# Gated linear attention and a gated SSM block: empty TensorE instructions behind 14 matmuls instead of 24, alpha's transpose ahead of the masks, v loaded ahead of q

## The chip, the cores and the metric

The kernel runs on one core of a Trainium2 chip. The metric is the device time of one execution in microseconds. A core has five engines with an instruction stream each, which meet only at semaphores: PE (TensorE, matmuls; its loads of the stationary operand are shown as PEld), DVE (VectorE), ACT (ScalarE), POOL (GpSimd) and SP (SyncE, which issues DMAs here). PE writes its results to PSUM, eight banks; DVE and ACT read them there.

## The reference, cut to what matters

Four batches, 8 heads, 768 steps, 48 channels a head. An attention with a state that decays by alpha, then a projection to two halves, a scan over one, a gate by the other, and an output projection.

```python
for t in range(S):
    state = alpha[:, :, t, :, None] * state + np.einsum('bhd,bhe->bhde', k[:, :, t], v[:, :, t])
    y[:, :, t] = np.einsum('bhd,bhde->bhe', q[:, :, t], state)
# x = y as (B, S, H * D)
proj = x @ w_in
val, gate = (proj[..., :D_inner], proj[..., D_inner:])
for t in range(S):
    h = a[0, 0] * h + val[:, t, :]
    ys[:, t, :] = h
silu = gate * (1.0 / (1.0 + np.exp(-gate)))
return (silu * ys @ w_out)
```

## The kernel before

The steps are cut into 12 groups of 256 (three for each batch), and a group is the unit of the outer loop in `fast`, `for n in range(N)`. The order on every engine is written out by hand: each engine runs its instructions in the order in which the Python code makes them, and there is no scheduler. A second function, `general`, is a way out for inputs that `fast` does not cover; it does not run here.

Three groups are in work in a turn n of the loop (for n from 2 on): the projection, gate and output of group n, the attention of group m = n + 1, and the preparation and the scores of group m + 1.

- **Preparation (DVE), `products`, lines 674 to 691.** A generator whose steps are taken one by one by `go(1)`: transpose alpha (`turn("a")`, tile al), transpose k, scan P of running products, scan V of the inverse ones (with `junk` on ACT), Zk = k x V, transpose q, Zq = q x P. `turn` is line 613.
- **Scores (PE), `scores`, line 816,** 64 matmuls of 64 x 112 from Zk and Zq into two pairs of PSUM banks, and **`masks`, lines 820 to 835:** DVE masks the first of each pair (A), ACT copies the second (AK) and the rest of the first (K), and POOL masks AK. ACT's copy K of a bank waits until DVE's mask of the same bank is done, and the second AK stands behind the first K on ACT.
- **Attention (PE), `third` and what surrounds it:** `carried` (L862), `values` (L849) and, for the next group, `states` (L881), which reads AK and K. `join` copies the result (ACT, L977, L978) and moves it between partitions by eight DMAs, four on SP's and four on POOL's queue, into xT.
- **Projection (PE), `project`, lines 997 to 1033:** four column blocks cc, six fp32 matmuls each (three for the value half, three for the gate half), all L1010; the scan hh on DVE (L1019) needs the first three of its block. The fourth scan is kept back (`late=True`) until Zq has been made, and behind it, with `f3`, stand the scores and masks of the group after.
- **Output (PE), `output_parts`,** 14 matmuls (L1095), whose sums are on DVE, POOL and ACT.

**Empty instructions.** Behind each projection matmul `project` puts `fill(n, cc, i)` instructions `nop` on PE (L1013). They compute nothing. `FILL` says how many there are for each group, and `fill` spreads them over the 24 matmuls:

```python
FILL = {1: 78, 2: 79, 3: 128, 4: 128, 5: 96, 6: 128, 7: 128, 8: 96, 9: 128}
count = FILL.get(n, 0)
at = 2 * NK * cc + i
return count * (at + 1) // 24 - count * at // 24
```

**Loads.** `load_raw` brings q, k or alpha of a group by four DMAs on SP's queue into one buffer for each of the three, so a load waits for the transpose that reads the buffer last. `load_v` brings v by two DMAs into one of two buffers in turn. SP issues in order: in a turn first the moves of `join`, then q, alpha, then in the next turn k, the output rows of the turn before and v.

Of the kernel before, what the change touches and what calls it, by code (L numbers as in the profile page):

```python
# [342 lines left out]
FIRST_PRODUCT = 1e18  # L343
FLOOR = 1e-31
FILL = {1: 78, 2: 79, 3: 128, 4: 128, 5: 96, 6: 128, 7: 128, 8: 96, 9: 128}


@with_exitstack
def fast(
# [25 lines left out]
    nc = tc.nc  # L375
# [7 lines left out]
    N = B * NG  # L383
# [50 lines left out]
    def load_v(m, engine):  # L434
        if m >= N:
            return
        b, g = divmod(m, NG)
        for c in range(G):
            if m:
                to = vs[m % NV][:, c, :, 0:D]  # L440
            else:
                to = wide[:, c].rearrange("p (h d) -> p h d", d=D)[:, ::2, :]
            engine.dma_start(out=to, in_=v[b, :, ds(g * GC + c * C, C), :].rearrange("h p d -> p h d"))
# [361 lines left out]
    def scores(m, cs=range(G)):  # L805
        Zk, Zq = Zks[m], Zqs[m % 2]
        for c in cs:
            scs.setdefault(m, []).append(bank_pair(None if c else "s"))
            if not c or not m:
                sts.setdefault(m, []).extend(scs[m][c])  # L810
            for p in range(4):
                for h in range(2):
                    u = 2 * c + h
                    for i in range(2):
                        rows = ds(64 * i, D)
                        nc.tensor.matmul(scs[m][c][i][ds(L * h, L), ds(p * (L + D), L + D)],  # L816
                                         Zk[rows, c, p, ds(h * L, L)], Zq[rows, u, p],
                                         start=True, stop=True, skip_group_check=True)

    def masks(m, cs=range(G)):  # L820
        sc = [[t[:, 0:4 * (L + D)].rearrange("p (h x) -> p h x", h=4) for t in pair] for pair in scs[m]]
        mb = mask[:, None, :]
        if m < NG:
            for c in cs:
                for i in range(2):
                    nc.vector.tensor_mul(As[i][:, c], sc[c][i][:, :, D:], mb.to_broadcast([C, 4, L]))
                for i in range(2):
                    nc.scalar.activation((K0, dS[m % 2][1])[i][:, c, :, 0:D], sc[c][i][:, :, 0:D], AF.Copy)
            return
        for c in range(G):  # L830
            nc.vector.tensor_mul(A0s[m % 2][:, c], sc[c][0][:, :, D:], mb.to_broadcast([C, 4, L]))
            nc.scalar.activation(AKs[m % 2][:, c], sc[c][1], AF.Copy)
            nc.scalar.activation(K0[:, c, :, 0:D], sc[c][0][:, :, 0:D], AF.Copy)
            t = AKs[m % 2][:, c, :, D:]
            nc.gpsimd.tensor_mul(t, t, mb.to_broadcast([C, 4, L]))
# [127 lines left out]
    for h in range(H):  # L963
        i, e, s = h // 4, h % 4 // 2, h % 2 ^ h // 4
        at = D * h
# [26 lines left out]
    def fill(n, cc, i):  # L992
        count = FILL.get(n, 0)
        at = 2 * NK * cc + i
        return count * (at + 1) // 24 - count * at // 24

    def project(n, cc, late=False, between=None):
        if cc == 0:
# [243 lines left out]
    for n in range(N):  # L1242
        m = n + 1
        if n == 0:
            V = scan_V(1, P)
            high(1)
            fs_late = [project(n, 0)]
            add_low(1)
            alphas(2)
            scaled_k(1, tk, V)  # L1250
            scaled_q(1, tq, P)
            low(2)
            fs_late.append(project(n, 1))
            convert(2)
            first(m)
            tk = straighten(2, "k")
            P = scan_P(2)
            tq = straighten(2, "q")
            V = scan_V(2, P)
            low(3)  # L1260
            convert(3)
            load_raw("k", 3, nc.sync)
            junk(1)
            def across_and_states():
                values(m, True)
                add_banks(m, states(m))

            f2 = project(n, 2, between=across_and_states)
            nc.scalar.activation(wobits[0][0:1, 0, 0, 0:1], minus[0:1], AF.Relu)
            load_w_out(0, nc.sync)  # L1270
            alphas(3)
            third(m)
            load_w_out(1, nc.sync)
            for name in "qa":
                load_raw(name, 3 + (name == "a"), nc.sync)
            load_v(3, nc.sync)
            for c in range(G):
                scaled_k(2, tk, V, c)
                scaled_q(2, tq, P, c)
        elif n == 1:  # L1280
            scores(m)
            masks(m)
            h3, f3 = project(0, 3, True)
            f2()
            P = scan_P(3)
            h3()
            values(m, True)
            st = states(m)
            add_banks(m, st)
            for f in fs_late:  # L1290
                f()
            f3()
            f0 = project(n, 0)
            convert(4)
            junk(2)
            low(5)
            convert(5)
            f1 = project(n, 1)
            f0()
            tk = plain("k")  # L1300
            turn("k", tk)
            third(m)
            load_raw("k", 4, nc.sync)
            load_v(4, nc.sync)
            f1()
            junk(3)
            V = scan_V(3, P)
            f2 = project(n, 2)
            scaled_k(3, tk, V)
            f2()  # L1310
            check_w(4)
            output(0)
            sum_weights()
            f3 = project(n, 3)
            tq = plain("q")
            turn("q", tq)
            load_raw("q", 4, nc.sync)
            scaled_q(3, tq, P)
            f3()
            go(2)  # L1320
        else:
            if n == 2:
                go(1)
            else:
                if m + 1 < N:
                    go(1)
                    load_raw("k", n + 3, nc.sync)
                go(1)
                next(outs, None)
                load_v(m + 1, nc.sync)  # L1330
            if n == N - 2:
                check_w(5)
            f0 = project(n, 0)
            f0()
            go(1)
            if n == 2:
                load_raw("a", n + 3, nc.sync)
                load_raw("k", n + 3, nc.sync)
            if n == N - 2:
                check_w(1)  # L1340
            f1 = project(n, 1)
            f1()
            sum_early()
            if n == 2:
                values(m, True)
                states(m)()
                add_up(m)
            if n == N - 2:
                check_w(2)
            go(1)  # L1350
            f2 = project(n, 2)
            f2()
            if n == N - 1:
                sum_last(0)
            if n == N - 2:
                check_end()
            go(1)
            if n == N - 1:
                tc.mark_branch_hint_location("last", hint=0, engines=[mybir.EngineType.PE, mybir.EngineType.Activation, mybir.EngineType.DVE, mybir.EngineType.SP, mybir.EngineType.Pool])
                value = nc.values_load(flag[0:1, 0:1], min_val=0, max_val=1)  # L1360
            h3, f3 = project(n, 3, True)
            if m + 1 < N:
                go(1)
            h3()
            f3()
            if m + 1 < N:
                scores(m + 1)
                masks(m + 1)
            if n == N - 3:
                check_w(3)  # L1370
            if n < N - 1:
                sum_late()
            else:
                sum_last(1)
            if m < N:
                rest = third(m)
                load_raw("q", n + 3, nc.sync)
                if m + 1 < N and m not in apart:
                    evict = states(m + 1)
                    values(m + 1, True)  # L1380
                go(1)
                if n + 3 < N:
                    load_raw("a", n + 4, nc.sync)
                rest()
                outs = output_parts(n)
                next(outs)
                if m + 1 < N and m not in apart:
                    evict()
                next(outs)
                if m in apart:  # L1390
                    values(m + 1, True)
                    states(m + 1)()
                if m + 1 < N:
                    add_up(m + 1)
            if n == N - 3:
                check_w(0)
        if n == N - 2:
            check_flag()
        if n == 1:
            output(n)  # L1400
            first(m + 1)
# [53 lines left out]
```

## Time and profile before

| | us |
|---|---|
| median of three runs | 284.66 |
| lowest and highest | 284.0, 284.67 |
| the profiled execution | 284.6 |
| its span, first to last instruction | 282.9 |
| busy: PE, PEld, DVE, POOL, ACT | 264.6, 232.7, 238.6, 158.9, 112.6 |
| the projections' matmuls L1010, into mm and into y | 103.6, 27.5 |

A busy PE is not a PE at its peak, since matmuls are pipelined and their ends are modelled. An fp32 matmul stands in the trace as two loads and two passes, so the 24 matmuls of one projection are x48. Instructions that only a sequencer handles, the empty ones among them, count as no engine's work: they are found by their line alone. "issue" is time in which an engine waited for nothing that the profile shows. One turn of the loop takes some 21 us; its scores start at 107.30, 128.86, 151.40, 172.23, 193.42, 215.70 and 236.52 us.

### The profile page before, as it was taken

To read this page: it belongs to the slowest core of one execution; us is meant where nothing else is said; L and a number is where in the kernel's file an instruction comes from. 1 tells how busy PE (TensorE), PEld (TensorE's weight loads), DVE (VectorE), ACT (ScalarE), POOL (GpSimd) and SP (SyncE) were. 2 spreads that over 40 slices of the span, in tenths; PEclk is the share of its full clock that TensorE was granted. 3 is DMA by queue.
4 is the path that set the end of the run, shared out by engine and by line. 5 is a ranking of instruction groups with operands and counts; after the bars stand their busy time and mean duration, and the time that the engine had idled before them with its cause. 6 is when DMAs were issued, how large, how long until landed. Compare 5 with 4: busy or idle time off the path is not lost.

```text
span 282.9 us, 11027 instructions
## 1 busy us (share of the span) xinstructions
PE 264.6 (94%) x4172; PEld 232.7 (82%) x4172; DVE 238.6 (84%) x326; ACT 112.6 (40%) x272; POOL 158.9 (56%) x195
## 2 busy tenths in 40 slices
PE   8999999999997997997997998997997997999995
PEld 6988888866786986986886987986886986988884
DVE  6979998998998898898698898898888988593452
ACT  3658665541524334334432533433423523414121
POOL 8122222445458884864695795775695795636110
PEclk9999999999999999999999999999999999999999
DMA  6937975989940693693594495594495460110201
GB/s 188 311 120 231 285 164 155 270 164 246 228 93 6 151 228 95 167 236 69 135 218 119 111 223 140 142 215 117 122 217 136 105 157 2 46 56 21 80 5 58
DMA packets 52308, 41.25 MB, mean 146 GB/s; under 512 B 27392, under 2 KB 50944, under 8 KB 52256
## 3 DMA queue, kind: packets, MB, share of 16 engines
q1 hardware_dynamic: 49472, 37.53, 54.9%
q0 software_dynamic: 1536, 2.20, 2.9%
q10 hardware_dynamic: 1248, 0.79, 1.0%
q8 instruction: 37, 0.61, 0.9%
q14 instruction: 15, 0.12, 0.1%
HBM read 32.54 MB, written 4.72 MB: 132 GB/s over the span
## 4 chain that ended last, share of the span: by engine, by line
PE 52%; DVE 30%; issue 6%; DMA 6%; ACT 2%; SPq 1%; POOL 1%; DVEq 0%; ACTq 0%; POOLq 0%
PE mm L1010 14%; PE mm L1095 14%; DVE q L613 6%; DVE V L667 6%; DMA raw_k<-in_k_dram 5%; DVE hh L1019 5%; DVE Zq L623 4%; PE s L816 3%; PE mm L816 3%; PE y L1095 3%; PE s L881 3%; PE y L862 2%; DVE P L648 2%; PE y L849 2%; DVE Zk L632 2%
## 5 line engine op out<-in xcount | busy, mean ns | idle before, releaser
L1010 PE MATMUL mm<-xT,w_in 128*128 128x256 f32 x456 | 103.6, 382 | 0.1
L1010 PEld LDWEIGHTS mm<-xT,w_in 128*128 128x128 f32 x456 | 85.5, 190 | 12.4 <-POOL w_in L569 0.4
L1032 POOL TENSOR_TENSOR f_last<-sg,hh 128x256 f32<-128x256 f32 x36 | 40.3, 1121 | 33.1 <-DVE hh L1019 21.9
L1030 ACT ACTIVATE sg<-mm 128x256 f32<-128x256 f32 x38 | 14.5, 382 | 84.3 <-PE mm L1010 84.3
L980 POOL DMA_DIRECT2D xT<-yst x44 | 22.5, 517 | 12.7 <-ACT yst L977 12.4
L667 DVE TENSOR_TENSOR_SCAN V<-al,ends 128x1028 f32<-128x1028 f32 x12 | 29.1, 2422 | 0.4
L648 DVE TENSOR_TENSOR_SCAN P<-al,lower 128x1028 f32<-128x1028 f32 x12 | 27.5, 2291 | 0.3
L1010 PE MATMUL y<-xT,w_in 128*128 128x256 f32 x120 | 27.5, 379 | 0.0
L1019 DVE TENSOR_TENSOR_SCAN hh<-a_dec,hh,mm 128x256 f32<-128x256 f32 x26 | 19.2, 738 | 8.1 <-PE mm L1010 8.1
L1010 PEld LDWEIGHTS y<-xT,w_in 128*128 128x128 f32 x120 | 22.8, 190 | 3.1
L569 POOL TENSOR_TENSOR w_in<-w_in,wr 128x768 int32<-128x768 int32 x4 | 7.3, 1823 | 26.1 <-DVE wr L564 16.2
L903 POOL TENSOR_TENSOR sum<-sum,dS 128x192 f32<-128x192 f32 x30 | 18.6, 621 | 2.0
L613 DVE STREAM_TRANSPOSE k<-raw_k 128x1024 f32<-128x1024 f32 x9 | 18.2, 2024 | 0.0
L613 DVE STREAM_TRANSPOSE q<-raw_q 128x1024 f32<-128x1024 f32 x9 | 18.2, 2024 | 0.0
L1120 POOL TENSOR_TENSOR wide_S<-wide_S,wr 128x192 f32<-128x192 f32 x9 | 15.1, 1674 | 5.6 <-ACT wr L1103 5.5
L1095 PE MATMUL mm<-w_out,f_last 128*128 128x192 f32 x80 | 17.5, 341 | 0.1
L1095 PE MATMUL mm<-wide,wr 128*128 128x192 f32 x88 | 17.2, 327 | 0.4 <-issue 0.4
L816 PEld LDWEIGHTS s<-Zq,Zk 48*64 48x64 f32 x384 | 9.6, 133 | 8.5 <-PE y L1010 3.6
L613 DVE STREAM_TRANSPOSE al<-raw_a 128x1024 f32<-128x1024 f32 x8 | 16.4, 2050 | 0.0
L632 DVE TENSOR_TENSOR Zk<-k,V 128x1024 f32<-128x1024 f32 (+1 forms) x14 | 16.1, 1147 | 0.1
L816 PE MATMUL s<-Zq,Zk 48*64 48x112 f32 x384 | 11.9, 261 | 4.4 <-DVE Zq L623 4.4
L623 DVE TENSOR_TENSOR Zq<-q,P 128x1024 f32<-128x1024 f32 (+1 forms) x14 | 15.4, 1102 | 0.3
(222 smaller groups left out, 550.7 us busy)
## 6 DMA issues: line engine op xcount, KB each, us to landing
out_dram<-o_sb SPq DMA_DIRECT2D x23, 192.0 KB, 4.9
v<-in_v_dram SPq DMA_DIRECT2D x22, 192.0 KB, 5.0
raw_k<-in_k_dram SPq DMA_DIRECT2D x18, 184.0 KB, 5.8
raw_q<-in_q_dram SPq DMA_DIRECT2D x18, 184.0 KB, 3.9
raw_k<-in_k_dram SPq DMA_DIRECT2D x18, 176.0 KB, 5.8
raw_q<-in_q_dram SPq DMA_DIRECT2D x18, 176.0 KB, 4.3
wbits<-in_moe_w_in_dram SPq DMA_DIRECT2D x8, 384.0 KB, 5.2
raw_a<-in_alpha_dram SPq DMA_DIRECT2D x16, 184.0 KB, 5.8
```

Of the source, the lines that this page charges most:

```text
L613: nc.vector.transpose(out=by_runs(to).rearrange("p h c j -> p h j c"), in_=raws[name][:, 0:4 * ROW].rearrange("p (h j d) -> p h j d", h=4, ...
L623: nc.vector.tensor_mul(Zqs[m % 2][:, ds(u0, n), :, D:].rearrange("p u h t -> p h u t"), t[:, :, at].rearrange("p h (u t) -> p h u t", t=L) ...
L632: nc.vector.tensor_mul(Zks[m][:, ds(c0, n)].rearrange("p c h t -> p h c t"), t[:, :, at].rearrange("p h (c t) -> p h c t", t=C), V[:, :, 1 ...
L648: nc.vector.tensor_tensor_scan(out=P, data0=al[:, 0:4 * GP], data1=lower.rearrange("p h t -> p (h t)"), initial=0.0, op0=ALU.mult, op1=ALU ...
L667: nc.vector.tensor_tensor_scan(out=V[:, ::-1], data0=al[:, 1:4 * GP + 1][:, ::-1], data1=ends.rearrange("p h t -> p (h t)")[:, ::-1], init ...
L816: nc.tensor.matmul(scs[m][c][i][ds(L * h, L), ds(p * (L + D), L + D)], Zk[rows, c, p, ds(h * L, L)], Zq[rows, u, p], start=True, stop=True ...
L903: nc.gpsimd.tensor_add(Ss[j][:, :, 0:D], Ss[j - 1][:, :, 0:D], part)
L980: engines[n % len(engines)].dma_start(out=xT[to, a], in_=st[rows, i, e])
L1010: nc.tensor.matmul((pv, pg)[vg], w_ins[cc][:, kk, vg, :], xT[:, kk, :], start=(kk == 0), stop=(kk == NK - 1))
L1019: nc.vector.tensor_tensor_scan(out=hh, data0=a_dec[:, cc:cc + 1].to_broadcast([C, GC]), data1=pv, initial=prev_h[cc][:, GC - 1:GC] if n % ...
L1032: f = lambda: engine.tensor_mul(fs[n][cc], sg, hh)
L1095: nc.tensor.matmul(o, a[:, k], b[k] if type(b) is list else b[:, k], start=start and k == 0, stop=k == KC - 1, skip_group_check=True)
```

## The change

The empty instructions keep their numbers and stand behind the first 14 of a group's 24 projection matmuls. The call `go(1)` that transposes alpha stands ahead of `masks(m + 1)` and no longer behind the moves of `join` and the loads. `load_v` is called in `third`'s turn for group m + 2, behind the moves and ahead of q, and no longer at the head of the next turn for the same group; so it is issued earlier by the loads of q, alpha and k and the output rows.

```diff
+FILLED = 14
...
         count = FILL.get(n, 0)
         at = 2 * NK * cc + i
-        return count * (at + 1) // 24 - count * at // 24
+        first = FILLED
+        return count * min(at + 1, first) // first - count * min(at, first) // first
...
                 go(1)
                 next(outs, None)
-                load_v(m + 1, nc.sync)
...
             f3()
             if m + 1 < N:
                 scores(m + 1)
+            go(1)
+            if m + 1 < N:
                 masks(m + 1)
...
                 rest = third(m)
+                load_v(m + 2, nc.sync)
                 load_raw("q", n + 3, nc.sync)
                 if m + 1 < N and m not in apart:
                     evict = states(m + 1)
                     values(m + 1, True)
-                go(1)
                 if n + 3 < N:
                     load_raw("a", n + 4, nc.sync)
```

PE, the head of the projection of group 6 (128 empty instructions), before:

```order
1050 L1010 MATMUL mm<-xT,w_in_96 128x256
1051 L1013 NO_OP x5
1052 L1010 MATMUL mm<-xT,w_in_96 128x256
1053 L1013 NO_OP x5
1054 L1010 MATMUL mm<-xT,w_in_96 128x256
1055 L1013 NO_OP x6
1056 L1010 MATMUL mm<-xT,w_in_96 128x256
```

and the end of the run of empty instructions in the same projection now, up to the scores (the lines are those of the changed file):

```order
984 L1012 MATMUL mm<-xT,w_in_97 128x256
985 L1015 NO_OP x9
986 L1012 MATMUL mm<-xT,w_in_98 128x256
987 L1015 NO_OP x9
988 L1012 MATMUL mm<-xT,w_in_98 128x256
989 L1015 NO_OP x10
990 L1012 MATMUL mm<-xT,w_in_98 128x256 x4
991 L1012 MATMUL mm<-xT,w_in_99 128x256 x6
992 L817 MATMUL s_3097<-Zq_117,Zk 64x112
```

Before, five or six stand behind each of the 24 matmuls; now nine or ten stand behind each of the first 14, and the last ten matmuls follow each other.

DVE, the turn of group 3, from the third scan to P, before:

```order
135 L1019 SCALAR_TENSOR_TENSOR hh<-a_dec,mm 128x256
136 L613 STREAM_TRANSPOSE q<-raw_q 128x4x8x32
137 L623 TENSOR_TENSOR Zq_118<-q,P 128x4x4x64
138 L1019 SCALAR_TENSOR_TENSOR hh<-a_dec,y_1876 128x256
139 L831 TENSOR_TENSOR A_114<-s_1922,mask 128x256
140 L831 TENSOR_TENSOR A_114<-mm,mask 128x256
141 L1083 TENSOR_TENSOR wr<-f_last,wr 128x256
142 L1084 TENSOR_TENSOR wr<-f_last,wr 128x256
143 L613 STREAM_TRANSPOSE al_129<-raw_a 128x4x8x32
144 L613 STREAM_TRANSPOSE k<-raw_k 128x4x8x32
```

and now:

```order
137 L624 TENSOR_TENSOR Zq_118<-q,P 128x4x4x64
138 L1021 SCALAR_TENSOR_TENSOR hh<-a_dec,y_1908 128x256
139 L614 STREAM_TRANSPOSE al_129<-raw_a 128x4x8x32
140 L832 TENSOR_TENSOR A_114<-s_1922,mask 128x256
141 L832 TENSOR_TENSOR A_114<-mm,mask 128x256
142 L1085 TENSOR_TENSOR wr<-f_last,wr 128x256
143 L1086 TENSOR_TENSOR wr<-f_last,wr 128x256
144 L614 STREAM_TRANSPOSE k<-raw_k 128x4x8x32
```

The transpose of alpha passes the two masks and the two sums for the output. This is so in turns 2 to 8; later turns have no alpha left to transpose.

SP, the same turn, between the moves of two groups, before:

```order
77 L980 DMA xT<-yst 48x256
78 L416 DMA raw_q<-in_q_dram 32x4x368
82 L416 DMA raw_a<-in_alpha_dram 32x4x368
86 L416 DMA raw_k<-in_k_dram 32x4x368
90 L1127 DMA out_dram<-o_sb 128x384 x2
91 L443 DMA v_94<-in_v_dram 128x8x48 x2
92 L980 DMA xT<-yst 48x256
```

and now (of four rows for each of q, alpha and k the first is shown, here and above):

```order
77 L981 DMA xT<-yst 48x256
78 L444 DMA v_94<-in_v_dram 128x8x48 x2
79 L417 DMA raw_q<-in_q_dram 32x4x368
83 L417 DMA raw_a<-in_alpha_dram 32x4x368
87 L417 DMA raw_k<-in_k_dram 32x4x368
91 L1129 DMA out_dram<-o_sb 128x384 x2
92 L981 DMA xT<-yst 48x256
```

The two DMAs of v pass the output rows and twelve loads.

## The prediction

> **What bounds the kernel now.** I read the page first (shares, clock, chain), then the chain of waits over one turn of the loop, then the timelines of DVE and PE in the same stretch, and last the instructions of single lines, which also show those that only the sequencer handles.
>
> ```profile
> span 282.9 us, 11027 instructions
> PE 264.6 (94%) x4172; PEld 232.7 (82%) x4172; DVE 238.6 (84%) x326; ACT 112.6 (40%) x272; POOL 158.9 (56%) x195
> PEclk9999999999999999999999999999999999999999
> PE 52%; DVE 30%; issue 6%; DMA 6%; ACT 2%; SPq 1%; POOL 1%; DVEq 0%; ACTq 0%; POOLq 0%
> ```
>
> The path to the end alternates between PE and DVE; the clock is full throughout. One turn, from the scores of one group (151.40) to those of the next (172.23), 20.8 us, in the chain:
>
> ```profile
> 151.40 1.00 PE s L816 x32
> 152.40 0.77 PE mm L816 x32
> ...
> 154.09 0.96 issue
> ...
> 155.51 0.74 PE s L881 x61
> ...
> 156.73 4.82 PE mm L1095 x28
> 161.55 1.31 PE mm L1010 x6
> ```
>
> PE holds the path from the scores to the third matmul of the projection (L1010; a matmul in fp32 is two passes, so x6 is three). From there DVE holds it, in program order:
>
> ```profile
> 162.88 0.69 DVE L1019 TENSOR_TENSOR_SCAN hh<-a_dec,mm 128x256 f32<-128x256 f32 x1 [0.87 <-PE mm L1010]
> ...
> 164.15 2.43 DVE L667 TENSOR_TENSOR_SCAN V<-al,ends 128x1028 f32<-128x1028 f32 x1
> 166.51 0.65 DVE L1019 TENSOR_TENSOR_SCAN hh<-a_dec,mm 128x256 f32<-128x256 f32 x1
> 167.09 1.19 DVE L632 TENSOR_TENSOR Zk<-k,V 128x1024 f32<-128x1024 f32 x1
> 168.20 0.67 DVE L1019 TENSOR_TENSOR_SCAN hh<-a_dec,mm 128x256 f32<-128x256 f32 x1
> 168.80 2.03 DVE L613 STREAM_TRANSPOSE q<-raw_q 128x1024 f32<-128x1024 f32 x1
> 170.86 1.22 DVE L623 TENSOR_TENSOR Zq<-q,P 128x1024 f32<-128x1024 f32 x1
> 172.00 0.68 DVE L1019 TENSOR_TENSOR_SCAN hh<-a_dec,mm 128x256 f32<-128x256 f32 x1
> 161.38 10.52 PE L1010 MATMUL mm<-xT,w_in 128*128 128x256 f32 x48
> 172.23 1.00 PE L816 MATMUL s<-Zq,Zk 48*64 48x112 f32 x32 [0.32 <-DVE Zq L623]
> ```
>
> The reader should see how even the two are: the 24 matmuls end at 171.9, Zq at 172.1, and PE idles 0.32 us between. Each scan L1019 needs three finished matmuls of its column block, and q and Zq stand behind the third scan on DVE. So a projection has no room to become longer.
>
> **The change, part by part.** *Empty instructions.* Their number per group stays (128 in groups 3, 4, 6, 7, 9; 96 in 5 and 8; 78 and 79 in 1 and 2); they move from behind 24 matmuls to behind 14. What one costs is read from the rows of their line, for group 6 (whole set, then its first run, with nothing between), and for group 5:
>
> ```profile
> L1013 PEldq NOP  x128: 13/13/13, 160.0 to 170.5; - x128
> L1013 PEldq NOP  x5: 13/13/13, 160.0 to 160.3; - x5
> L1013 PEldq NOP  x96: 13/13/13, 139.9 to 148.1; - x96
> L1010 PE MATMUL mm<-xT,w_in x48: 379/379/379, 161.4 to 171.5; 128*128 128x256 f32 x48
> ```
>
> Each is recorded with 13 ns, but the starts tell the price: four steps in 0.3 us, about 75 ns, and 10.5 us / 127 = 83 ns when the matmuls' own instructions and waits lie between. The array takes 10.1 us / 47 = 0.216 us a pass, 0.431 us a matmul. With 128/24 = 5.3 behind each, the sequencer needs 5.3 x 0.075 = 0.40 us and some issue time for each 0.431 us: it just keeps up, from a lead of 1.4 us (160.0 against 161.4). With 128/14 = 9.1 it needs 0.69 us or more, and matmuls behind an empty instruction cannot be issued before it. The fifteenth matmul has all 128 ahead of it. Bounds: 128 x 0.075 = 9.6 us, and the 10.5 us that the whole set took with ten matmuls more. Issue of those ten is 40 instructions; the 64 score matmuls with their loads, 128 instructions, passed in 1.00 + 0.77 us, at most 14 ns each, so 0.55 us, which leaves 9.95. I take 9.8: the fifteenth starts at 160.0 + 9.8 = 169.8 and not at 161.4 + 14 x 0.431 = 167.4, **2.4 us late**.
>
> [...] The rows above show 75 ns.
>
> The fifteenth matmul completes the third block, whose scan started at 168.20. Before, its last pass (number 30) ended at 161.4 + 29 x 0.216 + 0.38 = 168.0, so 0.2 us of slack: scan, q and Zq come 2.2 us late. The first scan is spared by the lead (third matmul issued at 160.0 + 2 x 0.7 = 161.4, due 162.3); the second block is 0.8 us late with 1.1 us of slack (167.09 - 0.65 against its pass 18 at 165.4). PE ends at 169.8 + 10 x 0.431 + 0.2 = 174.3, together with Zq. Two of the five groups have a little more slack; I take 2.1 each, **10.5 us**.
>
> Groups 5 and 8, with 96:
>
> ```profile
> 140.00 2.86 PE L1010 MATMUL mm<-xT,w_in 128*128 128x256 f32 x12
> 141.60 0.75 DVE L1019 TENSOR_TENSOR_SCAN hh<-a_dec,hh,mm 128x256 f32<-128x256 f32 x1 [2.36 <-PE mm L1010]
> 147.31 0.73 DVE L1019 TENSOR_TENSOR_SCAN hh<-a_dec,hh,mm 128x256 f32<-128x256 f32 x1
> ```
>
> No lead here (139.9 against 140.0). The fifteenth waits for 96 x 0.075 = 7.2 to 8.2 us; 7.4 taken: it starts at 147.3, not at 140.1 + 6.0 = 146.1; 1.2 us late, minus 0.55 of slack (ready at 140.1 + 29 x 0.216 + 0.38 = 146.75, scan at 147.31): 0.65 each, **1.3 us**. Groups 1 and 2 get 5.6 a matmul, 0.42 us: nothing, hidden under the 0.431.
>
> *Alpha ahead of the masks* (groups 2 to 8, seven times). DVE's al transpose now fills the wait for the scores, and the masks, with ACT's copies K, which wait for them, and POOL's mask behind ACT, move back:
>
> ```profile
> 151.17 0.74 DVE L1019 TENSOR_TENSOR_SCAN hh<-a_dec,hh,y 128x256 f32<-128x256 f32 x1
> 152.44 0.42 DVE L831 TENSOR_TENSOR A<-s,mask 128x256 f32<-128x256 f32 x1 [0.53 <-PE s L816]
> 153.20 0.42 DVE L831 TENSOR_TENSOR A<-mm,mask 128x256 f32<-128x256 f32 x1 [0.34 <-PE mm L816]
> ...
> 154.90 2.06 DVE L613 STREAM_TRANSPOSE al<-raw_a 128x1024 f32<-128x1024 f32 x1
> 152.48 0.54 ACT L832 ACTIVATE AK<-s 128x448 f32<-128x448 f32 x1 [1.36 <-PE s L816]
> ...
> 153.72 0.33 ACT L833 ACTIVATE K<-mm 128x192 f32<-128x192 f32 x1
> 153.10 1.60 POOL L835 TENSOR_TENSOR AK<-AK,mask 128x256 f32<-128x256 f32 x2 [0.32 <-ACT AK L832]
> ```
>
> DVE would save 0.53 + 0.34 = 0.87 us. But its next dependence is the first scan, which idles 0.87 (group 6) or 2.36 us (group 5) for PE: it would only idle longer. Gain at most 7 x 0.87 = 6.1, taken 0. Loss: al ends at 151.9 + 2.0 = 153.9 (the scan ahead, from 151.17, ends at 151.9), the masks at 154.3 and 154.7, the last K copy, behind the second AK copy, at 155.4 instead of 154.05, POOL's second half at 155.9. PE's states (L881) run from 155.51 and need the second K in their second half, from 155.9; what covers the shift is the 0.96 us for which PE stands still before L862. Without that cover it costs up to 1.4 us a group, 9.8 in all; taken 0.
>
> *v ahead of q* on SP's queue, one group earlier:
>
> ```profile
> 159.53 2.13 SPq L416 DMA_DIRECT2D raw_q<-in_q_dram  x4
> 161.75 3.16 SPq L416 DMA_DIRECT2D raw_a<-in_alpha_dram  x4
> ...
> 168.51 1.29 SPq L443 DMA_DIRECT2D v<-in_v_dram  x2
> raw_q<-in_q_dram SPq DMA_DIRECT2D x18, 176.0 KB, 4.3
> raw_a<-in_alpha_dram SPq DMA_DIRECT2D x2, 176.0 KB, 5.2
> 161.38:172.23 10.85, 10.53 (x50) 8.97 (x49) 9.87 (x12) 2.50 (x6) 8.24 (x9) 1.00 1.06 238
> ```
>
> Two issues (1.3 us) and 384 KB at 238 GB/s (1.6 us) now pass ahead of q, alpha and k; output rows and the next turn's moves follow as before. v waits for matmuls that end before the moves ahead of it. raw_q, due at 168.80, was issued until 161.7 and landed 4.3 us later, at 166.0, then at 167.6: enough. raw_a, issued until 164.9, landed 5.2 us later, at 170.1, then at 171.7; alpha's turn is now due at 172.7, not 175.7. It fits by 1.0 us, by 3.2 with the projection longer. Cost 0; without the cover up to 1 us a group, 7 in all.
>
> **Sum.** Against the profiled execution's 284.6 us (span 282.9; the median of the runs is 284.66, the same): 284.6 + 10.5 + 1.3 = **296.4; I forecast 296.5 us**.
>
> **The rivals.** *Hidden: no change, 284.6.* The empty instructions would not hold the matmuls back. [...] Against it: equal steps of 75 ns, and a sequencer only 1.4 us ahead. 9%. *Faster, 278.5.* As before hidden, and DVE's 0.87 us reach the end seven times: 284.6 - 6.1. It needs PE to be early too, and the first scan waits for PE in every group; 5%. *Masks late, 301.5.* The forecast, and alpha's transpose on the path through masks, ACT and POOL to L881 or L849: it decides where PE's stop before L862 shrinks below about 0.5 us, or where raw_a lands after 174. Half of 9.8 on top: 296.5 + 5. For it: 0.3 to 0.5 us of margin; against it: PE's stop is 0.96 us here and no cause of it is moved. 9%. My forecast has the remaining 77%.
>
> **How the numbers follow.** The forecast's own range: with 9.6 us for the 128, 0.2 less in five groups and in two, 295; with 10.5 and 8.2 us, 0.7 x 5 + 0.8 x 2 more, 301.5; slack that I misread by 0.3 us moves either end by 2. So 293 to 301.5 alone. The range of 8 in 10 is 291 to 302: it leaves out the two rivals on the other side (14%) and part of the third. About 0.3% (0.85 us) is what a measurement of this kernel can tell from no change: faster 0.05, same 0.09, slower 0.86.
>
> **What would show it.** Sets of L1010 that last about 13 us in the five groups with 128 and some 11.8 with 96, gaps in the first fourteen matmuls and none in the last ten; DVE idle before the third scan for about 2 us, released by PE; L1013's rows 128 in 9.5 to 10 us with steps of 75 ns still; in groups 10 and 11, which have none, no change. Alpha: no idle before masks, more idle before the first scan, L881 at the same distance from the scores. Wrong would be: L1010 sets of 10.5 us (then they are hidden), or stops before L881 or L849 released by ACT or POOL, or DVE waiting for raw_a.

## The result, and the profile after

The changed kernel takes 297.51 us in the median (297.29 to 298.12, four runs), the kernel before 284.51 (284.0 to 284.67, four runs): a ratio of 1.0464 [1.0442, 1.0486], 13 us slower. The profiled execution took 298.12 us with a span of 296.0, where the kernel before has 282.9; the difference of the spans is 13.1 us, and it is this that is taken apart below.

The page of the changed kernel: span, busy time, the chain by engine, and the group of the projection's weight loads (busy us, mean ns, idle time before them and what ended most of it).

```profile
span 296.0 us, 11020 instructions
PE 279.5 (94%) x4172; PEld 225.9 (76%) x4172; DVE 233.0 (79%) x326; ACT 112.2 (38%) x272; POOL 139.3 (47%) x195
PEclk9999999999999999999999999999999999999999
PE 51%; DVE 19%; DMA 16%; issue 6%; SPq 4%; ACT 1%; POOL 1%; DVEq 0%; POOLq 0%; ACTq 0%
L1012 PEld LDWEIGHTS mm<-xT,w_in 128*128 128x128 f32 x456 | 80.9, 190 | 28.5 <-issue 16.4
```

PE's own row misleads: its busy time rose by 15 us to the same 94%, because a pass is recorded with 0.38 us and at full rate the next one starts 0.22 us after its start: passes that stand apart overlap less. The loads of the weights show it: they stood idle for 16.4 us "for issue" ahead of the projection's matmuls, that is, for nothing that the profile shows. In the timeline of PEld over the projection of group 6 (start, duration, and in brackets the idle time ahead), four matmuls run at full rate, then ten stand apart, then ten follow without a gap:

```profile
165.92 1.65 PEld L1012 LDWEIGHTS mm<-xT,w_in 128*128 128x128 f32 x8
167.78 0.30 PEld L1012 LDWEIGHTS mm<-xT,w_in 128*128 128x128 f32 x2 [0.21 <-issue]
168.44 0.30 PEld L1012 LDWEIGHTS mm<-xT,w_in 128*128 128x128 f32 x2 [0.36 <-issue]
...
174.05 0.30 PEld L1012 LDWEIGHTS mm<-xT,w_in 128*128 128x128 f32 x2 [0.36 <-issue]
174.82 4.18 PEld L1012 LDWEIGHTS mm<-xT,w_in 128*128 128x128 f32 x20 [0.47 <-issue]
```

The fifth matmul comes at 167.78 and the fifteenth at 174.82: 0.704 us each where the array needs 0.431. The rows of the empty instructions' line, for group 6 and for group 5, end when the gaps end:

```profile
L1015 PEldq NOP  x128: 13/13/13, 164.7 to 174.8; - x128
L1015 PEldq NOP  x96: 13/13/13, 143.6 to 151.2; - x96
```

The timelines of DVE and PE in the same stretch show whom this delays:

```profile
168.57 2.30 DVE L668 TENSOR_TENSOR_SCAN V<-al,ends 128x1028 f32<-128x1028 f32 x1
171.35 0.69 DVE L1021 TENSOR_TENSOR_SCAN hh<-a_dec,mm 128x256 f32<-128x256 f32 x1 [0.48 <-PE mm L1012]
171.96 1.20 DVE L633 TENSOR_TENSOR Zk<-k,V 128x1024 f32<-128x1024 f32 x1
175.56 0.69 DVE L1021 TENSOR_TENSOR_SCAN hh<-a_dec,mm 128x256 f32<-128x256 f32 x1 [2.40 <-PE mm L1012]
176.16 2.02 DVE L614 STREAM_TRANSPOSE q<-raw_q 128x1024 f32<-128x1024 f32 x1
178.21 1.23 DVE L624 TENSOR_TENSOR Zq<-q,P 128x1024 f32<-128x1024 f32 x1
166.08 13.32 PE L1012 MATMUL mm<-xT,w_in 128*128 128x256 f32 x48
179.58 1.00 PE L817 MATMUL s<-Zq,Zk 48*64 48x112 f32 x32 [0.18 <-DVE Zq L624]
```

DVE had no idle time between V and the third scan before; now it stands 0.48 us before the second scan and 2.40 us before the third, both times for PE, and q, Zq and the scores follow. The set of 24 matmuls lasts 13.32 us instead of 10.52.

The chain of waits gives DMA 16% now (6% before), and in this turn it runs through two loads:

```profile
166.57 4.83 DMA raw_q<-in_q_dram
...
171.41 4.73 DMA raw_k<-in_k_dram
...
176.16 2.03 DVE q L614
```

This is not a new bound. The transpose of q starts 0.60 us behind the start of the third scan (176.16 against 175.56), and it did so before (168.80 against 168.20): it follows the instruction ahead of it on DVE, and k happens to land at that moment. In groups 3 to 9 of both kernels the distance is 0.60 or 0.66 us, so the load holds it up in none of them.

The seven turns between the scores of the first group with 128 and those of the last, by the starts of the first projection matmul and of the scores:

| stretch | forecast | spans |
|---|---|---|
| first matmul to scores, five groups with 128 | +10.5 us | +12.8 |
| first matmul to scores, two groups with 96 | +1.3 | +1.9 |
| scores to first matmul, seven turns | 0 | -1.3 |
| ahead of these turns and behind them | 0 | -0.3 |
| sum | +11.8 | +13.1 |

The groups 10 and 11, without empty instructions, have sets of 10.52 and 10.63 us as before.

### The profile page after: what moved, and what is told of

Same layout as the page of the kernel before. It is cut to its first block, busy times and chain, and to the rows that moved or that the text cites. A ratio compares the mean times of both kernels' runs of the same rounds, so it can differ in the third digit from the quotient of the medians.

```text
span 296.0 us, 11020 instructions
## 1 busy us (share of the span) xinstructions
PE 279.5 (94%) x4172; PEld 225.9 (76%) x4172; DVE 233.0 (79%) x326; ACT 112.2 (38%) x272; POOL 139.3 (47%) x195
## 4 chain that ended last, share of the span: by engine, by line
PE 51%; DVE 19%; DMA 16%; issue 6%; SPq 4%; ACT 1%; POOL 1%; DVEq 0%; POOLq 0%; ACTq 0%
PE mm L1012 14%; PE mm L1097 11%; DMA raw_k<-in_k_dram 10%; DVE q L614 5%; DMA raw_q<-in_q_dram 5%; DVE Zq L624 4%; PE s L817 3%; PE y L1012 3%; SPq L417 3%; PE mm L817 3%; PE y L863 3%; DVE V L668 2%; DVE P L649 2%; PE s L882 2%; PE y L1097 2%
## 5 line engine op out<-in xcount | busy, mean ns | idle before, releaser
L1012 PE MATMUL mm<-xT,w_in 128*128 128x256 f32 x456 | 113.3, 391 | 1.3
L1012 PEld LDWEIGHTS mm<-xT,w_in 128*128 128x128 f32 x456 | 80.9, 190 | 28.5 <-issue 16.4
L1034 POOL TENSOR_TENSOR f_last<-sg,hh 128x256 f32<-128x256 f32 x36 | 31.8, 883 | 62.8 <-ACT sg L1032 43.4
L1012 PE MATMUL y<-xT,w_in 128*128 128x256 f32 x120 | 31.9, 394 | 0.7
L1012 PEld LDWEIGHTS y<-xT,w_in 128*128 128x128 f32 x120 | 20.9, 189 | 10.7 <-issue 8.0
L668 DVE TENSOR_TENSOR_SCAN V<-al,ends 128x1028 f32<-128x1028 f32 x12 | 28.2, 2348 | 0.4
L614 DVE STREAM_TRANSPOSE al<-raw_a 128x1024 f32<-128x1024 f32 x8 | 16.4, 2055 | 0.0
L1021 DVE TENSOR_TENSOR_SCAN hh<-a_dec,mm 128x256 f32<-128x256 f32 x12 | 8.2, 681 | 10.3 <-PE mm L1012 10.3
L1097 PEld LDWEIGHTS mm<-wide,wr 128*128 128x128 f32 x88 | 14.7, 190 | 0.7 <-issue 0.7
```

The costliest lines, as they stand in the source:

```text
L614: nc.vector.transpose(out=by_runs(to).rearrange("p h c j -> p h j c"), in_=raws[name][:, 0:4 * ROW].rearrange("p (h j d) -> p h j d", h=4, ...
L668: nc.vector.tensor_tensor_scan(out=V[:, ::-1], data0=al[:, 1:4 * GP + 1][:, ::-1], data1=ends.rearrange("p h t -> p (h t)")[:, ::-1], init ...
L1012: nc.tensor.matmul((pv, pg)[vg], w_ins[cc][:, kk, vg, :], xT[:, kk, :], start=(kk == 0), stop=(kk == NK - 1))
L1021: nc.vector.tensor_tensor_scan(out=hh, data0=a_dec[:, cc:cc + 1].to_broadcast([C, GC]), data1=pv, initial=prev_h[cc][:, GC - 1:GC] if n % ...
L1034: f = lambda: engine.tensor_mul(fs[n][cc], sg, hh)
L1097: nc.tensor.matmul(o, a[:, k], b[k] if type(b) is list else b[:, k], start=start and k == 0, stop=k == KC - 1, skip_group_check=True)
```

## The experiments

Each kernel ran beside the kernel before on the same chip. That kernel's median was 284.45 us beside the first four and 285.35 to 285.65 beside the others, so ratios are what compares. Twelve kernels ran, in the order of the questions below.

**The empty instructions alone** (fill14):

```diff
-        return count * (at + 1) // 24 - count * at // 24
+        first = 14
+        return count * min(at + 1, first) // first - count * min(at, first) // first
```

> The kernel before, with the empty instructions put behind the first 14 matmuls and nothing else changed. Theory (PE's sequencer is kept up by 9.1 empty instructions per matmul, so the third scan's matmul comes late): the whole loss stands here, 284.5 + 12 to 13 = 296.5 to 297.5 us; the first-pass sets of the 128-groups last 13.3 us, those of the 96-groups 12.1. Rival (the moved turn of alpha or the moved load of v carries a part of the loss): this kernel stays 2 us or more below the changed one, at 295.5 us or less. Second rival (alpha or v wins something back that the empty instructions lose): it comes out above 298.5 us.

Measured: 298.07 us, ratio 1.0481 [1.0459, 1.0503], sets of 13.32 and 12.1 us. The whole loss is here, and a little more than the theory's range; the interval overlaps with that of the changed kernel, so whether the two moves win back the 0.2% between them is not told by these two.

**The moves alone** (alpha; v; both in alpha_v). Alpha is `go(1)` ahead of `masks(m + 1)`, v is `load_v(m + 2, nc.sync)` ahead of `load_raw("q", ...)`, as in the diff of the change; the empty instructions lie over all 24 matmuls.

> The kernel before, with only alpha's turn put ahead of the masks; the empty instructions lie over all 24 matmuls and v's load stands where it stood. Theory (alpha's turn is off the path that sets the end): 283.5 to 285.5 us, and the first-pass sets unchanged at 10.5 us. Rival (the masks come late behind alpha's turn on ACT and hold the scores' consumers): 287 us or more, with idle time of DVE or PE before the masks. Second rival (the first scan gets its input earlier and the group shortens): 283 us or less.

> The kernel before, with only v's load moved behind the start of third and one step ahead of the other tensors. Theory (the load has landed long before it is used in either place): 284.0 to 285.0 us. Rival (it delays the transfers of q, k and a that stand behind it in SP's queue): 286 us or more, with DMA waits before the turns of q, k or a.

> The kernel before, with alpha's turn and v's load both moved and the empty instructions over all 24 matmuls: the change without its first part. Theory (the two moves are free): 283.5 to 285.5 us. Rival (they cost together, since v's issue and alpha's turn now stand in the same stretch): 287 us or more. Second rival (they win together, and the loss of the empty instructions hid it): 283 us or less.

Measured: alpha 0.9961 [0.9946, 0.9976], 283.43 us; v 0.9999 [0.9985, 1.0012]; both 0.9978 [0.9964, 0.9992]. v is free. Alpha is not nothing: it wins 0.2 to 0.5%, some 1 us, which lies between the theory and its second rival, and its sets stay at 10.5 us. A difference that was not expected shows on DVE and POOL after the masks. First the kernel before, then alpha, the same turn, timelines of DVE and POOL:

```profile
179.73 2.30 DVE L648 TENSOR_TENSOR_SCAN P<-al,lower 128x1028 f32<-128x1028 f32 x1
181.95 0.33 DVE L1122 TENSOR_TENSOR wr<-wide,y 128x192 f32<-128x192 f32 x1
180.28 2.13 POOL L1120 TENSOR_TENSOR wide_S<-wide_S,wr 128x192 f32<-128x192 f32 x1 [0.69 <-ACT wr L1103]
```

```profile
176.73 2.30 DVE L648 TENSOR_TENSOR_SCAN P<-al,lower 128x1028 f32<-128x1028 f32 x1
180.52 0.35 DVE L1122 TENSOR_TENSOR wr<-wide,y 128x192 f32<-128x192 f32 x1 [1.49 <-PE y L1095]
178.95 0.58 POOL L1120 TENSOR_TENSOR wide_S<-wide_S,wr 128x192 f32<-128x192 f32 x1 [0.68 <-ACT wr L1103]
```

DVE no longer waits for the scores ahead of the masks and reaches P 1.7 us earlier in the turn (7.5 us behind the start of the scores at 172.23 before, 5.8 behind 170.90 now). POOL's sum L1120 then falls behind P instead of beside it and takes 0.58 us instead of 2.13; beside P it ended 0.4 us after P. The nine instructions of this line take 15.1 us in the kernel before and 5.5 in alpha. P itself takes 2.30 us in both turns; what slows the sum beside it, the rows do not show. And L1122, which followed P without a gap, now waits 1.49 us for PE. How much of the 1 us comes from there was not separated: the stop of PE ahead of the carried product, below, is also 0.9 us shorter over the eight turns of alpha's profile.

**How much the empty instructions may be bunched** (fill17 and fill20: `first = 17`, `first = 20` in the lines of fill14). The 71 ns in what was expected is the step between the starts of empty instructions that follow each other directly; in the changed kernel's trace 468 of 610 such steps have this length, and none is below 70 ns.

> The same 128 and 96 empty instructions, behind the first 17 matmuls: 7.5 and 5.6 per matmul. Theory (128 at 71 ns from the first one on, and the array waits where its matmul has not been reached): the 18th matmul of a 128-group comes 1.0 us late, the 15th 0.6 us, so the third scan is late by some 0.5 us and the scores by 0.5 to 1.0; the 96-groups lose nothing (5.6 x 71 ns = 0.40 us, below 0.431). 5 x 0.5 to 1.0 = 2.5 to 5: 287 to 289.5 us. Rival (any bunching costs the 12 us): 294 us or more. Second rival (the loss needs the full 9.1 per matmul): 285.5 us or less.

> The same 128 and 96 empty instructions, behind the first 20 matmuls: 6.4 and 4.8 per matmul. Theory: the 128 take 128 x 71 ns + 0.9 us for the matmuls between them = 10.0 us from the first one on, and the array reaches its 21st matmul 10.1 us after the first empty instruction even before the change; so nothing is late although 6.4 x 71 ns = 0.45 us is above the 0.431 us of a matmul: sets of 10.5 to 10.7 us and 284 to 285.5 us in all. Rival (the rate per matmul alone decides, not the lead that the sequencer has at the start): 5 x 0.5 or more, 287 us or more.

Measured: fill17 1.0136 [1.0064, 1.0209], that is 284.5 + 1.8 to 5.9 us; fill20 0.9973 [0.9935, 1.0011]. The loss goes from 13.7 to 4 to none as the same 128 instructions are spread over 14, 17 and 20 matmuls, as the sum over the sequencer's time gives it, and against both rivals of fill17 and the one of fill20. fill17's weight loads in group 6, and its set:

```profile
165.98 0.30 PEld L1011 LDWEIGHTS mm<-xT,w_in 128*128 128x128 f32 x2 [0.29 <-issue]
...
171.26 2.89 PEld L1011 LDWEIGHTS mm<-xT,w_in 128*128 128x128 f32 x14 [0.31 <-issue]
162.47 12.08 PE L1011 MATMUL mm<-xT,w_in 128*128 128x256 f32 x48
```

From the ninth matmul (165.98) to the eighteenth (171.26) it is 5.28 / 9 = 0.587 us each with 128 / 17 = 7.53 empty instructions; in the changed kernel 0.704 with 9.14. These two give slope and rest, 0.117 / 1.61 = **0.073 us for an empty instruction and 0.04 for the matmul's own instructions**, an estimate from two densities. For fill20 this makes 6.4 x 0.073 + 0.04 = 0.51, above 0.431 again, and its set is indeed 10.9 us long, 0.4 more than before and 0.2 more than expected; but the lag comes after the fifteenth matmul, DVE is not behind, and the scores are not late. In fill17 the set grew by 1.56 us and not by the 1.0 expected, since that sum had no term for the matmuls themselves, up to 0.7 us for 17 at 0.04.

**Half as many** (fill14_half: the lines of fill14, and 64 and 48 in place of 128 and 96):

```diff
-FILL = {1: 78, 2: 79, 3: 128, 4: 128, 5: 96, 6: 128, 7: 128, 8: 96, 9: 128}
+FILL = {1: 78, 2: 79, 3: 64, 4: 64, 5: 48, 6: 64, 7: 64, 8: 48, 9: 64}
```

> Behind the first 14 matmuls as in the change, but half as many empty instructions in groups 3 to 9 (64 and 48 in place of 128 and 96): 4.6 and 3.4 per matmul. Theory (what counts is how long PE's sequencer takes per matmul): 4.6 x 71 ns = 0.33 us is below the 0.431 us of a matmul, so the first-pass sets are back at 10.5 us and the third scan is not late; the total, with the instructions of a turn no longer 768, 283 to 288 us. Rival (instructions only in the first 14 places hurt by their position, whatever their number): half the loss stays, 290 us or more, with sets of 11.5 us or more.

Measured: 0.9898 [0.9837, 0.9958]; the set of group 6 lasts 10.52 us. The place behind the first 14 matmuls cost nothing in itself here. That it is 0.4 to 1.6% faster than the kernel before was not expected. Its trace has 4.8 us of the stops of PE behind the scores that are taken up below, and the kernel before 8.1; the size fits, but no run tests this alone.

**The same density at the other end** (last14):

```diff
-        return count * (at + 1) // 24 - count * at // 24
+        skip, over = 10, 14
+        return count * max(at + 1 - skip, 0) // over - count * max(at - skip, 0) // over
```

> The kernel before, with the 128 and 96 empty instructions behind the last 14 matmuls in place of all 24: the same 9.1 and 6.9 per matmul as in the change, at the other end. Theory (each matmul waits until PE's sequencer has passed what stands before it): the 15th matmul comes up to 4 x (0.69 - 0.43) = 1.0 us late and the last one up to 14 x 0.26 = 3.6 us, less what the sequencer is ahead of the array at the 11th; the scores follow the last matmul, so a 128-group loses 1 to 3.6 us and the total is 289 to 302 us. Rival (the sequencer can run far ahead in ten matmuls without empty instructions): 286 us or less. Second rival (dense empty instructions only hurt at the start, where the third scan waits): as before, 284 to 285 us.

Measured: 0.9986 [0.9953, 1.0018], no loss. The time fits both rivals; that it is the first is read from the rows of its empty instructions and of its set in group 6:

```profile
L1014 PEldq NOP  x128: 13/13/13, 164.1 to 173.8; - x128
163.20 10.56 PE L1011 MATMUL mm<-xT,w_in 128*128 128x256 f32 x48
```

The first empty instruction, behind the eleventh matmul, passes the sequencer 0.9 us after the array took the first one. So the sequencer is 10 x 0.431 - 0.9 = 3.4 us ahead there. The last matmul has 13 of the 14 portions ahead of it, and 13 x (0.704 - 0.431) = 3.5 us of lag use the lead up just there: the set is 0.04 us longer, and 0.11 at most in the other groups with 128. The density is that of the changed kernel (0.704 us a matmul there); what differs is the lead that the sequencer has to spend, 3.4 us at the first empty instruction here and 1.4 there (164.7 against 166.08).

**Whether they are of use in the kernel before** (nofill: `FILL = {}`; shift: 64 fewer in groups 1 and 2; shift_alpha: the same with alpha).

```diff
-FILL = {1: 78, 2: 79, 3: 128, 4: 128, 5: 96, 6: 128, 7: 128, 8: 96, 9: 128}
+FILL = {1: 14, 2: 15, 3: 128, 4: 128, 5: 96, 6: 128, 7: 128, 8: 96, 9: 128}
```

> No empty instructions at all, in any group. Theory (in the kernel before they are hidden behind the array, and their use is to fix where PE's instruction fetches fall): sets unchanged at 10.5 us, and the total 284 to 290 us, with PE's idle time for issue falling at other places from turn to turn. Rival (they cost the kernel before part of its time): 282 us or less, with shorter sets or an earlier first matmul.

> The kernel before with 64 empty instructions fewer in each of groups 1 and 2 (14 and 15 in place of 78 and 79), groups 3 to 9 as before: every block of 256 instructions that PE fetches (16 KB each) then begins 128 instructions later in each later turn, with the number per turn kept. It asks why the run without empty instructions was faster than the kernel before. Theory (PE's idle time for issue ahead of the carried product, 8 x 1.0 us in the kernel before, comes from where a block begins): most of it goes or falls under other work, 278 to 283 us. Rival (the empty instructions of groups 3 to 9 themselves cost it): 284 to 285 us, less than 1 us for the ones left out.

> The same as shift, with alpha's turn ahead of the masks as well. Theory (the two act in different stretches and add): 1.0 us below shift. Rival (alpha's turn only gained where the idle time for issue left room): as shift, within 0.3 us.

Measured: nofill 0.9927 [0.9892, 0.9962], shift 0.9882 [0.9838, 0.9927], shift_alpha 0.9938 [0.9907, 0.9969]. PE's waits for issue behind the scores (us in total, times, longest), of the kernel before, of the changed one, of nofill and of shift:

```profile
PE mm L862 <- issue: 4.2, 4, 1.3
PE y L862 <- issue: 3.9, 4, 1.1
```

```profile
PE mm L863 <- issue: 3.5, 4, 1.0
PE y L863 <- issue: 3.0, 4, 0.9
```

```profile
PE s L881 <- issue: 2.6, 3, 1.2
PE mm L862 <- issue: 2.2, 3, 0.8
PE y L849 <- issue: 1.2, 1, 1.2
```

```profile
PE s L881 <- issue: 6.5, 6, 1.5
```

With the same count in each turn, the stop stands at the same instruction in all eight turns (L862); without them it wanders; with 64 fewer in each of groups 1 and 2 it stands at L881. Counted in the traces, each of these stops stands, in every run, at an instruction of PE that has 193 or 194 more than a multiple of 256 ahead of it. A turn of the kernel before has 768, three times 256, so the stop keeps its place; a turn of nofill has 640 or 672. The page counts 37 instruction packets of 16 KB (0.61 MB), and PE's 9445 instructions make 36.9 blocks of 256; in nofill it is 34 packets and 33.0 blocks. The stops last 0.4 to 1.5 us, yet in these four runs each ends 1.2 to 1.6 us after the end of such a packet. A wait of PE for a block of its instructions to be fetched would fit these counts and times; no row names the cause.

nofill falls between its two cases: its sets are not shorter (10.5 us), as the theory said, and the total is lower, as the rival said; the 0.7% (2.1 us) match the shorter stops behind the scores, 6.0 us in all instead of 8.1. In shift 6.5 us remain, so the stop moved and shrank but did not go: the time lies in the theory's range, and its reason holds for 1.6 us of 8.1. The profiled execution of shift cannot show the whole 1.2% (3.4 us), since it took 284.76 us, the longest of six with a median of 282.49. In it the turns are 2.0 us shorter (148.06 us from the scores at 88.40 to those at 236.46, where the kernel before takes 150.06 from 86.46 to 236.52), of which the stops are 1.6; what lies ahead of these turns is as much longer.

shift_alpha failed both of its cases: it is not below shift but, if anything, above (the intervals overlap). In its trace the wait stands that the prediction named as the risk of alpha's move, and that no trace with the stop at L862 shows:

```profile
PE mm L1095 <- ACT K L833: 1.6, 2, 0.8
PE s L881 <- ACT K L833: 0.9, 3, 0.3
```

**The changed kernel with half as many** (after_half: the `FILL` of fill14_half, and all three parts of the change).

> The changed kernel with all its three parts, and half as many empty instructions in groups 3 to 9 (64 and 48 in place of 128 and 96). Theory (the whole loss is the time of the empty instructions ahead of the 15th matmul, and the two moves are free or better): sets back at 10.5 us, at or below the kernel before by 0.5 to 1.2%: 281 to 283.5 us beside 284.5. Rival (alpha's turn or v's load loses something that the empty instructions had covered in the changed kernel): 286 us or more.

Measured: 0.992 [0.9889, 0.995], 283.33 us beside 285.35. Sets are back at 10.5 us, here group 6:

```profile
161.07 10.52 PE L1012 MATMUL mm<-xT,w_in 128*128 128x256 f32 x48
```

It is faster than the kernel before and the changed one. Shift, fill14_half and after_half have overlapping intervals; which of them is the best is not told.

## Why the prediction was right

The forecast was 296.5 us and the median is 297.51, of 291 to 302.

**The mechanism, and its sign: right, and shown.** Empty instructions alone carry the loss (fill14), their number times their duration ahead of the fifteenth matmul sets it (fill14_half, fill17, fill20), and the lead of the sequencer is what hides them (last14). The rival in which they are hidden fell: 0.073 us each by the two densities, not the 0.013 of their record.

**Groups with 128: mechanism right, term too small.** Forecast 2.1 us each, measured 2.3 to 2.7, 12.8 in place of 10.5. The step that was mis-sized is "I take 9.8" for the fifteenth matmul: it came 10.1 us after the first empty instruction (164.7 to 174.82). Both bounds that 9.8 was taken between were too low. The lower one, 128 x 0.075 = 9.6, has no time for the fourteen matmuls that stay in the run; at 0.04 us each they make it 10.2. The upper one, 9.95, takes off 0.55 us for the ten matmuls that leave it; at 0.04 us each it is 0.4, which gives 10.1. The slack of 0.2 us ahead of the third scan was as read: the fifteenth matmul starts 2.7 us later and by the modelled ends is done 2.8 us later, and the scan comes 2.65 later (10.86 us after the first empty instruction, 8.2 before). The second scan was forecast to be spared and stood 0.48 us for PE: its block came 1.2 us late instead of 0.8, and DVE was ready 0.4 us sooner. This costs nothing, since DVE waits again at the third.

**Groups with 96: the same term.** Forecast 1.2 us late and 0.65 lost, measured 1.4 late (7.70 us after the first empty instruction in place of 6.28) and 0.97 lost in each.

**Groups 1 and 2: right.** The scores of the group ahead of the first with 128 start at 86.33 us, at 86.46 before.

**Alpha: cost right, gain missed.** The masks came late as worked out, and their cover held. ACT's copies K and PE's stop in the changed kernel:

```profile
156.50 2.05 DVE L614 STREAM_TRANSPOSE al<-raw_a 128x1024 f32<-128x1024 f32 x1
158.39 0.41 DVE L832 TENSOR_TENSOR A<-s,mask 128x256 f32<-128x256 f32 x1
158.90 0.33 ACT L834 ACTIVATE K<-s 128x192 f32<-128x192 f32 x1 [1.21 <-DVE A L832]
159.55 0.34 ACT L834 ACTIVATE K<-mm 128x192 f32<-128x192 f32 x1
159.74 0.47 PE L863 MATMUL mm<-Zq,sum 48*64 48x64 f32 x17 [0.99 <-issue]
160.03 0.21 PE L882 MATMUL s<-v,K 64*48 64x48 f32 x2
```

The last K ends at 159.89, 0.14 us before L882 starts and ahead of its use; without PE's stop of 0.99 us ahead of L863 it would not. That the stop is the cover is supported by shift_alpha and after_half, where in some turns it lies elsewhere and PE waits for K (2.5 and 1.4 us in all). What failed is "it would only idle longer" at the first scan: the time saved goes into waits for PE ahead of L1124 (1.72 us in this turn), and on the way it takes P away from POOL's L1120. Taken at 0, the move is worth some 1 us in the kernel before; in the changed one, which waits for PE, its share can't be told.

**v: right.** 0.9999, and no wait for a load.

**The total: nearer than its terms, by luck.** The two terms together were 3.0 us too small; 1.3 us came back between scores and projection, where the stop before the carried product is 6.5 us in eight turns and not 8.1. The forecast had 0 there. Fill14 has 7.1, and what shortens it was not tried. One slip lies in the forecast's own range: 2 us on either end of 295 to 301.5 gives 293 to 303.5, and only the lower end was moved.

## What to carry to other kernels

An instruction that computes nothing took its turn in the sequencer here, and its cost was read from the steps between its starts (0.071 us, where its record says 0.013). Per matmul, (instructions x their step) is compared with the array's time, 9.14 x 0.073 against 0.431 us in the changed kernel; what was over was paid out of the lead that the sequencer had built up (3.5 us of lag against 3.4 of lead in last14, whose set was 0.04 us longer), and then by whoever waited for that matmul (DVE for 2.40 us ahead of the third scan in the changed kernel). So filling belongs behind the matmuls that another engine waits for, or where the lead is long. And a stop that costs time by itself can be the cover of something else, as PE's stop of 0.99 us was for K, for which PE waited 2.5 us in shift_alpha: before it is removed, look at what would wait next.

## What the runs showed of the hardware

- An empty instruction on PE took 0.073 us of its sequencer and is recorded with 0.013; a matmul's own instructions took some 0.04 (estimates from 0.704 us a matmul in the changed kernel and 0.587 in fill17).
- PE's sequencer was 3.4 us, eight matmuls of 0.431 us, ahead of the array behind ten matmuls without empty instructions (last14).
- PE stopped for 0.4 to 1.5 us behind the scores in most turns, at 193 or 194 instructions above a multiple of 256 (all runs), and went on 1.2 to 1.6 us after the end of a 16 KB packet of instructions (before, changed kernel, nofill, shift).
- A POOL sum of 128 x 192 took 0.58 us behind DVE's running product of 128 x 1028 (alpha), and 2.13 beside it (before, the same turn).
